# Attention, then a routed expert layer on one core: token rows scattered to expert regions batch by batch, in place of an inverse permutation built from one-hots

## The chip, the core and the metric

The kernel runs on one core of a Trainium2 chip. A core has five engines that run at the same time and meet through semaphores: TensorE (PE; its weight loads are listed as PEld), VectorE (DVE), ScalarE (ACT), GpSimd (POOL) and SyncE (SP), which issues transfers. Each engine takes its own instructions strictly in the order in which they were built. Transfers run on 16 DMA engines, through queues. The metric is the device time of one execution in microseconds (us).

## The reference

The input is `q`, `k`, `v` of shape 8 x 8 x 576 x 64 (batch, head, token, width), a gate matrix 512 x 8, a local gate 512 x 1 and, for eight experts, `w1` of 512 x 1024 and `w2` of 1024 x 512.

1. Attention for each batch and head, scale 1/8. A token sees all tokens of its own block of 64 and of the blocks before it (9 blocks of 64).
2. The heads are joined: x is 8 x 576 x 512.
3. Routing, token by token and in order within a batch. `fresh` is the argmax of the eight gate logits. The first token of a batch, and every token whose local gate is under 0.5, takes `fresh`; any other token keeps the expert of the token before it.
4. out = p[e] * (relu(x @ w1[e]) @ w2[e]), where p is the softmax of the gate logits and e the token's expert.

4,608 tokens go to 8 experts; how many go to each is known only at run time.

## The kernel before, in words

**Attention.** There are 32 pairs of heads (four pairs to a batch) and a loop over i from -1 to 31. Iteration i turns the exponentials of pair i (`turn_p`, L519), makes the scores of pair i+1 (`scores`, L481, three groups), their row maxima on DVE (`maxima`, L505) and exponentials on ACT (`exps`, L513), turns q and k of pair i+2 (`turn`, L462), finishes pair i-1 (`finish`, L569: five matmuls that transpose the output and give gate logits, then four DVE multiplications by the inverse row sums `rv`), and multiplies by v (`attend`, L544; `inverse`, L560, computes `rv` with six reciprocals on DVE). The order of all of these within an engine is the program's order (`pin`). `finish` adds the logits on POOL to `lg_all` and writes the token rows through SP to the DRAM tensor `x_rows`. Sixteen weight loads `w_bf` (1 MB each) are issued from POOL behind `finish`, one every one or two iterations (L634).

**Routing** (`routing`, L145) is a generator of small steps. Part 0 covers batches 0 to 5 at once, part 1 the last two. MIDDLE and BEHIND (L601, L602) say after which iterations 24 to 31 a step of part 0 is taken; MIDDLE is between `finish` and the third score group, BEHIND after `inverse`. A step finds the argmax, carries the kept expert along the tokens by a scan (over two round trips through DRAM on SP's queue), ranks the tokens of each expert by matmuls with a triangle and with ones, and gives each token a slot in a list of tiles of 128 tokens, each of one expert. The inverse (slot to token) is then built by one-hots: per batch a 128 x 640 comparison on DVE (L336), a narrower one (L339), five multiplications (L343) and matmuls (L350), which give token number and gate value of each slot.

**Expert layer.** 43 tiles (20 of part 0, 23 of part 1). For each: an indirect gather of 128 rows from `x_rows` on POOL (L665), four transposes (`turn_x`, L671), a DVE copy `xb` (L677), a DVE copy of the expert's `w1` into `wt` (`fetch`, L687), 32 matmuls (`up`, L694), two relus, the second of them on DVE from tile 18 on (L706 to L709), eight matmuls (`down`, L711), an ACT scaling into `o_sb` (four buffers, L719), and an indirect scatter to the output on POOL (L720). Part 1's routing steps stand between the first tiles (L742), without `pin`. Each output scatter waits until the one before it has landed, since both write one DRAM tensor.

Of the kernel before, what the change touches and what calls it, by code (L numbers as in the profile page):

```python
# [16 lines left out]
def kernel(  # L17
# [11 lines left out]
    nc = tc.nc  # L29
# [38 lines left out]
    lg_all = w_p.tile([P, B * NJ, E + 1], F32, tag="lg_all", name="lg_all")  # L68

    x_dram = nc.dram_tensor("x_rows", [BS, Dm], BF16).ap()  # L70
# [4 lines left out]


    NB0 = 6
    NC0 = NB0 * NJ
    NT0 = -(-(NB0 * S - E * (P - 1)) // P)
    PARTS = [(0, NC0, NT0), (NC0, NC_, NT - NT0)]  # L80
    NTM = max(NT0, NT - NT0)

    OUT = 8192.0
# [12 lines left out]
    K = Const()  # L96

    def route_constants():
        K.id_b = rt([P, P], BF16, "id_b")
        nc.gpsimd.tensor_copy(K.id_b, id_f)  # L100
        K.iota_e = rt([P, E], F32, "iota_e")
        nc.gpsimd.iota(K.iota_e, pattern=[[1, E]], base=0, channel_multiplier=0,
                       allow_small_or_imprecise_dtypes=True)
        K.desc_e = rt([P, E], F32, "desc_e")
        nc.gpsimd.tensor_scalar(K.desc_e, K.iota_e, -1.0, float(E), op0=ALU.mult, op1=ALU.add)
        K.thr = rt([P, NTM], BF16, "thr")
        nc.gpsimd.iota(K.thr, pattern=[[1, NTM]], base=0, channel_multiplier=0,
                       allow_small_or_imprecise_dtypes=True)
        K.iota_lo = rt([P, P], BF16, "iota_lo")
        nc.gpsimd.iota(K.iota_lo, pattern=[[1, P]], base=0, channel_multiplier=0,  # L110
                       allow_small_or_imprecise_dtypes=True)
        K.ones_b = rt([P, P], BF16, "ones_b")
        nc.gpsimd.memset(K.ones_b, 1.0)

        tri_f = rt([P, P], F32, "tri_f", tag="big")
        nc.gpsimd.memset(tri_f, 1.0)
        nc.gpsimd.affine_select(out=tri_f, in_=tri_f, compare_op=ALU.is_gt, fill=0.0,
                                base=0, pattern=[[1, P]], channel_multiplier=-1)
        K.tri_b = rt([P, P], BF16, "tri_b")
        nc.gpsimd.tensor_copy(K.tri_b, tri_f)  # L120
        K.ones_e = rt([P, NC0 * E], BF16, "ones_e")
        nc.gpsimd.memset(K.ones_e, 1.0)

        K.val = rt([P, NC_, 5], BF16, "val")
        tmp = rt([P, NC_], F32, "chunk_id", tag="eqm")
        nc.gpsimd.iota(tmp, pattern=[[S // 64, B], [2, NJ]], base=0, channel_multiplier=0,
                       allow_small_or_imprecise_dtypes=True)
        nc.gpsimd.tensor_copy(K.val[:, :, 0], tmp)
        tmp = rt([P, 1], F32, "part1", tag="mx")
        nc.gpsimd.iota(tmp, pattern=[[0, 1]], base=1, channel_multiplier=1,  # L130
                       allow_small_or_imprecise_dtypes=True)
        nc.gpsimd.tensor_copy(K.val[:, :, 1], tmp.to_broadcast([P, NC_]))
        K.oh = rt([P, E, NC_], BF16, "oh")
        K.slot = rt([P, NC_], F32, "slot")
        K.off = rt([P, E], F32, "off")
        K.sub = rt([P, E], F32, "sub")
        K.taken = rt([P, E], F32, "taken")
        K.cnt = rt([P, E], F32, "cnt")

    pslots = [rt([P, x[2]], F32, "pslot%d" % k) for k, x in enumerate(PARTS)]  # L140
    tok_gs = [rt([P, x[2]], I32, "tok_g%d" % k) for k, x in enumerate(PARTS)]
    tok_ss = [rt([P, x[2]], I32, "tok_s%d" % k) for k, x in enumerate(PARTS)]
    te_is = [rt([1, x[2]], I32, "te_i%d" % k) for k, x in enumerate(PARTS)]

    def routing(k, ew, last, psum, pin):  # L145

        c0, c1, nt = PARTS[k]
        n = c1 - c0
        b0, b1 = c0 // NJ, c1 // NJ
        a_dram = nc.dram_tensor("a_dram%d" % k, [2, b1 - b0, NJ * P], BF16).ap()  # L150
        e_dram = nc.dram_tensor("e_dram%d" % k, [b1 - b0, NJ * P], BF16).ap()
        dve = nc.vector
        rows = [P, n, E]

        def ts(out, in_, a, b, op0=ALU.mult, op1=ALU.add):
            pin(dve.tensor_scalar(out, in_, a, b, op0=op0, op1=op1))

        def each(ap):
            return ap[:, :, None].to_broadcast([P, E, n])

        lg = lg_all[:, c0:c1, :E]
        mx = rt([P, n], F32, "mx")
        pin(dve.reduce_max(mx, lg, axis=AX))
        mx3 = mx[:, :, None].to_broadcast(rows)

        eqm = rt(rows, F32, "eqm")
        pin(dve.tensor_tensor(eqm, lg, mx3, op=ALU.is_ge))
        pin(ew.tensor_mul(eqm, eqm, K.desc_e[:, None, :].to_broadcast(rows)))
        ep = rt(rows, F32, "ep")
        pin(ew.tensor_sub(ep, lg, mx3))  # L170
# [3 lines left out]
        best = rt([P, n], F32, "best")  # L174
        pin(dve.reduce_max(best, eqm, axis=AX))
        ak = rt([P, 2, n], F32, "ak")
        pin(dve.tensor_single_scalar(ak[:, 1, :], lg_all[:, c0:c1, E], 0.0, op=ALU.is_ge))
        pin(dve.memset(ak[0:1, 1, 0:n:NJ], 0.0))
        ts(best, best, -1.0, float(E))
        nkeep = rt([P, n], F32, "nkeep")  # L180
        ts(nkeep, ak[:, 1, :], -1.0, 1.0)
        pin(dve.tensor_mul(ak[:, 0, :], best, nkeep))
# [5 lines left out]
        pin(nc.tensor.transpose(ps[:2 * n, :P], ak.rearrange("p a c -> p (a c)"), id_f))  # L188
        akT = rt([2 * n, P], BF16, "akT")
        pin(nc.scalar.copy(akT, ps[:2 * n, :P]))  # L190
        nc.sync.dma_start(out=a_dram.rearrange("a b (t p) -> (a b t) p", p=P), in_=akT)
        row = rt([b1 - b0, 2, S], BF16, "row", tag="ring", bufs=2)
        nc.sync.dma_start(out=row, in_=a_dram[:, :, :S].rearrange("a b s -> b a s"))
        sm = rt([P, n], F32, "sm")
# [5 lines left out]
        erow = rt([b1 - b0, NJ * P], BF16, "erow", tag="ring", bufs=2)  # L200
        pin(dve.memset(erow[:, S:], 0.0))
        pin(dve.tensor_tensor_scan(erow[:, :S], row[:, 1, :], row[:, 0, :], 0.0,
                                   op0=ALU.mult, op1=ALU.add))
        nc.sync.dma_start(out=e_dram, in_=erow)
        ecr = rt([n, P], BF16, "ecr", tag="akT")
        nc.sync.dma_start(out=ecr, in_=e_dram.rearrange("b (t p) -> (b t) p", p=P))
        yield

        ps = psum()
        pin(nc.tensor.matmul(ps[:, :n], lhsT=ecr, rhs=K.id_b[:n, :n], start=True, stop=True))  # L210
        eix = rt([P, n], F32, "eix", tag="best")
        pin(dve.tensor_copy(eix, ps[:, :n]))

        oh = K.oh[:, :, c0:c1]
        pin(dve.tensor_tensor(oh, eix[:, None, :].to_broadcast([P, E, n]),
                              K.iota_e[:, :, None].to_broadcast([P, E, n]), op=ALU.is_equal))
        pin(dve.memset(K.oh[64:, :, c0 + NJ - 1:c1:NJ], 0.0))

        pin(ew.tensor_mul(ep, ep, oh.rearrange("p e c -> p c e")))
# [4 lines left out]
        for x, m in enumerate((K.tri_b, K.ones_b)):  # L224
            pin(nc.tensor.matmul(ps[:, x * n * E:(x + 1) * n * E].rearrange(
                "p (e c) -> p e c", e=E), lhsT=m, rhs=oh, start=True, stop=True))
        rc = rt([P, 2, E, n], F32, "rc", tag="big")
        rc2 = rc.rearrange("p x e c -> p (x e c)")
        pin(nc.scalar.copy(rc2, ps[:, :2 * n * E]))
        pg = rt([P, n], F32, "pg")  # L230
        pin(dve.reduce_sum(pg, ep, axis=AX))
        pin(dve.tensor_mul(pg, pg, sm))
        pin(dve.tensor_copy(K.val[:, c0:c1, 2], pg))
        for j in (3, 4):
            pin(dve.tensor_sub(pg, pg, K.val[:, c0:c1, j - 1]))
            pin(dve.tensor_copy(K.val[:, c0:c1, j], pg))
        yield

        inc = rt([P, E, n], F32, "inc", tag="eqm")
        pin(dve.tensor_tensor_scan(inc.rearrange("p e c -> p (e c)"), K.ones_e[:, :n * E],  # L240
                                   rc[:, 1].rearrange("p e c -> p (e c)"), 0.0,
                                   op0=ALU.mult, op1=ALU.add))

        pin(dve.tensor_sub(inc, inc, rc[:, 1]))
        pin(dve.tensor_add(rc[:, 0], rc[:, 0], inc))
        cnt = rt([P, E], F32, "cnt_n")
        pin(dve.tensor_add(cnt, inc[:, :, n - 1], rc[:, 1, :, n - 1]))
        pin(dve.tensor_sub(cnt, cnt, inc[:, :, 0]))
        yield

        ci = rt([P, 2, E], I32, "ci")
        til = rt([P, E], F32, "til")
        end = rt([P, E], F32, "end")
        exc = rt([P, E], F32, "exc")
        base = rt([P, E], F32, "base")

        def tiles(c):
# [525 lines left out]
```

## Time and profile before

| quantity | value |
|---|---|
| median of 3 runs | 623.67 us (623.26 to 628.08) |
| profiled execution: device time / span | 625.85 / 623.8 us |
| busy PE / DVE / ACT / POOL | 563.6 / 452.7 / 329.4 / 155.3 us |
| granted TensorE clock, mean | 0.975 |
| first matmul of the scores (L492) | 13.86 us |
| first `turn_p` (L526) | 23.55 us |
| one iteration, from 204 to 304 us | 11.9 us |
| first matmul of `up` (L700) | 429.81 us |
| `up` of the last tile / last output scatter issued | 605.23 / 616.45 us |

The span runs from the first to the last instruction of the profiled execution. An engine's busy time does not tell whether it sets the pace; that is read from what ends its idle time. Ends of matmuls are modelled, so starts are compared here.

### The profile page before, as it was taken

To read this page: it belongs to the slowest core of one execution; us is meant where nothing else is said; L and a number is where in the kernel's file an instruction comes from. 1 tells how busy PE (TensorE), PEld (TensorE's weight loads), DVE (VectorE), ACT (ScalarE), POOL (GpSimd) and SP (SyncE) were. 2 spreads that over 40 slices of the span, in tenths; PEclk is the share of its full clock that TensorE was granted. 3 is DMA by queue.
4 is the path that set the end of the run, shared out by engine and by line. 5 is a ranking of instruction groups with operands and counts; after the bars stand their busy time and mean duration, and the time that the engine had idled before them with its cause. 6 is when DMAs were issued, how large, how long until landed. Compare 5 with 4: busy or idle time off the path is not lost. (4 is left out here: it accounts for less than half of the span.)

```text
span 623.8 us, 15804 instructions
## 1 busy us (share of the span) xinstructions
PE 563.6 (90%) x5586; PEld 396.2 (64%) x5586; DVE 452.7 (73%) x1403; ACT 329.4 (53%) x1057; POOL 155.3 (25%) x218
## 2 busy tenths in 40 slices
PE   2899999999999999999999998765989899999991
PEld 1567667677677677666766665554667677766660
DVE  1688888888888888888888788894588855555540
ACT  1676676666666676666666765601444343323320
POOL 3000010010000001001010010144565565666532
PEclk9999999999999999999999999986999999999996
DMA  8246596595958668695874746102232222222210
GB/s 165 55 96 115 116 158 117 120 177 102 170 123 158 103 131 163 114 182 109 153 136 96 136 90 113 23 10 61 78 104 77 99 89 78 94 91 90 82 56 0
DMA packets 154078, 65.99 MB, mean 106 GB/s; under 512 B 138010, under 2 KB 146226, under 8 KB 154002
## 3 DMA queue, kind: packets, MB, share of 16 engines
q0 software_dynamic: 18048, 31.86, 24.8%
q1 hardware_dynamic: 132466, 32.52, 24.2%
q10 hardware_dynamic: 3488, 0.61, 0.6%
q8 instruction: 46, 0.75, 0.5%
q14 instruction: 30, 0.25, 0.1%
HBM read 67.55 MB, written 16.02 MB: 134 GB/s over the span
## 5 line engine op out<-in xcount | busy, mean ns | idle before, releaser
L516 ACT ACTIVATE pb<-ps_s,nm 128x512 f32<-128x512 f32 (+4 forms) x320 | 158.3, 501 | 97.8 <-DVE nm L508 97.3
L508 DVE TENSOR_REDUCE nm<-ps_s 128x1 f32<-128x512 f32 (+4 forms) x320 | 134.5, 453 | 54.0 <-ACT pb L516 31.8
L526 PE MATMUL ps_p<-id_f,pb 128*128 128x128 f32 (+1 forms) x800 | 105.1, 282 | 11.4 <-ACT pb L516 8.0
L492 PE MATMUL ps_s<-kT,qT 64*64 64x512 f32 (+7 forms) x1280 | 100.7, 419 | 6.1 <-ACT qT L475 6.1
L526 PEld LDWEIGHTS ps_p<-id_f,pb 128*128 128x128 f32 (+1 forms) x800 | 86.3, 141 | 24.7 <-ACT pb L516 10.0
L590 POOL TENSOR_TENSOR tmp<-tmp 128x45 f32<-128x45 f32 x32 | 8.5, 264 | 356.9 <-DVE tmp L582 356.9
L700 PEld LDWEIGHTS <-wt 128*128 128x128 bf16 x1376 | 81.1, 98 | 21.1 <-issue 15.8
L553 PE MATMUL ps_o<-pt,vt 128*64 128x320 f32 (+4 forms) x896 | 93.6, 360 | 0.0
L700 PE MATMUL ps_h<-xb,wt 128*128 128x128 bf16 x1376 | 84.3, 220 | 9.3 <-DVE xb L677 9.1
L714 PE MATMUL ps_o<-w_bf,hT 128*128 x344 | 86.6, 379 | 0.4
L553 PEld LDWEIGHTS ps_o<-pt,vt 128*64 128x64 f32 x896 | 59.3, 137 | 35.8 <-DVE tmp L582 4.9
L707 ACT ACTIVATE hT<-ps_h 128x512 bf16<-128x512 f32 x61 | 36.4, 597 | 79.1 <-PE ps_h L700 79.1
L720 POOL DMA_INDIRECT out_dram<-o_sb,tok_s x43 | 54.5, 1268 | 63.8 <-DMA out_dram<-o_sb,tok_s 21.0
L492 PEld LDWEIGHTS ps_s<-kT,qT 64*64 64x64 f32 x1280 | 45.4, 134 | 38.2 <-issue 23.6
L691 DVE COPY wt<-w_bf 128x4096 bf16 x43 | 53.1, 1238 | 15.5 <-PE ps_h L700 13.0
L516 ACT ACTIVATION_READ_ACCUMULATOR pb<-ps_s,nm 128x1 f32 x320 | 64.3, 201 | 0.0
L665 POOL DMA_INDIRECT xg<-x_rows,tok_g x43 | 55.3, 1286 | 22.6 <-PE ps_x L674 9.3
L719 ACT ACTIVATE o_sb<-ps_o,pslot 128x512 f32<-128x512 f32 x43 | 29.5, 687 | 44.0 <-PE ps_o L714 38.3
L709 DVE TENSOR_SCALAR hT<-ps_h 128x512 bf16<-128x512 f32 x25 | 17.3, 691 | 48.1 <-PE ps_h L700 48.1
L578 PE MATMUL ps_n<-wg,ot 128*128 128x146 f32 x320 | 49.4, 303 | 0.0
L541 ACT COPY pt<-ps_p 64x128 f32<-64x128 f32 (+2 forms) x102 | 43.6, 441 | 10.5 <-PE ps_p L526 10.3
L714 PEld LDWEIGHTS <-hT 128*128 128x128 bf16 x344 | 31.2, 98 | 24.8 <-issue 1.1
(147 smaller groups left out, 568.7 us busy)
## 6 DMA issues: line engine op xcount, KB each, us to landing
w_bf<-in_moe_w_dram POOLq DMA_DIRECT2D x16, 1024.0 KB, 10.2
natq<-in_q_dram SPq DMA_DIRECT2D x64, 128.0 KB, 2.6
vt<-in_v_dram SPq DMA_DIRECT2D x64, 128.0 KB, 4.7
natk<-in_k_dram SPq DMA_DIRECT2D x60, 128.0 KB, 2.7
x_rows<-xt SPq DMA_DIRECT2D x32, 128.0 KB, 2.6
natq<-in_q_dram SPq DMA_DIRECT2D x32, 32.0 KB, 2.5
vt<-in_v_dram SPq DMA_DIRECT2D x32, 32.0 KB, 6.3
natk<-in_k_dram SPq DMA_DIRECT2D x30, 32.0 KB, 2.2
```

The costliest lines, as they stand in the source:

```text
L492: pin(nc.tensor.matmul(ps[y][f * 64:(f + 1) * 64, c:c + n], lhsT=qT[r, i * 64:(i + 1) * 64], rhs=kT[r, a:a + n], start=True, stop=True))
L508: pin(nc.vector.reduce_max(nm[:, z:z + 1], ps[g][y][:, c:c + n], axis=AX, negate=True))
L516: pin(nc.scalar.activation(pb[i][:, a:a + n], ps[g][y][:, c:c + n], func=AF.Exp, bias=nm[:, i:i + 1], accum_out=rs[:, z:z + 1]))
L526: pin(nc.tensor.transpose(ps[:kk, (c + e) * P:(c + e + 1) * P], pb[i0 + 2 * e][:, j * P:j * P + kk], id128))
L541: pin(cp(dst, src))
L553: pin(nc.tensor.matmul(ps[h * D:(h + 1) * D, a - q0:qn], lhsT=vts[i % 3][:, j, h, :], rhs=pt[j][:, h, a - j * P:a - j * P + n], start=(j = ...
L578: pin(nc.tensor.matmul(ps[:, (t - t0) * (P + WG):(t - t0 + 1) * (P + WG)], lhsT=ot[:, t * P:(t + 1) * P], rhs=wg[:, hp], start=True, stop= ...
L665: nc.gpsimd.indirect_dma_start(out=xg[:], out_offset=None, in_=x_dram[:rows], in_offset=bass.IndirectOffsetOnAxis(ap=tok_gs[k][:, u:u + 1] ...
L691: nc.vector.tensor_copy(wt.rearrange("p k f -> p (k f)"), w1_bf[:, bass.ds(o, WE)])
L700: nc.tensor.matmul(ps_h[:, f, :], lhsT=wt[:, ko, fo * P:(fo + 1) * P], rhs=xb[:, ko * P:(ko + 1) * P], start=(ko == 0), stop=(ko == KO1 - 1))
L714: nc.tensor.matmul(ps_o, lhsT=hT[:, fo, :], rhs=w2_bf[:, bass.ds(woff + fo * Dm, Dm)], start=(fo == 0), stop=(fo == FO - 1))
L720: nc.gpsimd.indirect_dma_start(out=out_flat, out_offset=bass.IndirectOffsetOnAxis(ap=tok_ss[k][:, u:u + 1], axis=0), in_=o_sb[:], in_offse ...
```

## The change

Tokens are no longer sorted at the end; each batch's rows are put into place as soon as its routing is known.

* A DRAM tensor `x_sorted` (`xs`) holds one region of 4,608 rows for each expert. A row has 512 bf16 values, the token number and the gate value: 258 words.
* `finish` writes the token rows into an SBUF tile `x_b` of the batch (two buffers: batch b+2 takes the buffer of batch b), not to DRAM. The new `routing` runs once per batch, in nine steps that `hook` takes at nine places of the following iterations; `hook(i, 0)` stands where MIDDLE stood, `hook(i, 1)` where BEHIND stood. `K.free` holds the next free row of each region. The last two steps issue five indirect scatters (rows of 128 tokens) on POOL, L259.
* `table(0)` works out, from the counts of six batches alone, 16 tiles of full rows (part 0) and their row numbers; `table(1)` the other 27. A gathered row brings its token number and gate value along.
* The first three gathers are issued in iteration 30, the other 13 of part 0 right behind the last `finish`. Routing of batch 7 and the rest of batch 6 stand between the first tiles, on DVE.
* `inverse` makes one reciprocal on DVE and copies to `rv` with six POOL instructions. The v tiles have two buffers, not three. At the start the ACT queue issues three transfers, not ten, and loads the table of the exponential at once; gate weights and k of pair 1 go through SP. The second relu goes to DVE from tile 14.

In the built program, with the line numbers of the changed kernel, the five scatters c0 to c4 of a batch stand on POOL like this (batch 0; iteration 8 and the beginning of iteration 9):

```
L343 w_bf load
L259 c0
L532 L533 L534 L532 L533 L534   rv copies of pair 8; the fourth waits for c0's landing
L259 c1
L259 c2          waits for c1's landing
L169 L171 L173   step 1 of batch 1
L259 c3          waits for c2's landing
L259 c4          waits for c3's landing
L559 logits of finish(8)
```

For batches 1 and 2, c0 and c1 both stand ahead of the `rv` copies, and the fourth copy waits for c1. A `w_bf` load stands directly ahead of c0 for batches 0, 3, 4 and 5. On DVE, the first L554 of `finish` (pair 8 for batch 0) waits for the landing of all five scatters, since batch 2 takes the buffer of batch 0.

```diff
+    ROW = Dm // 2 + 2
+    xs = nc.dram_tensor("x_sorted", [E * BS, ROW], I32).ap()
+    PARTS = [NB0 * S // P - E - 3, 0]
+    PARTS[1] = NT - PARTS[0]
...
+    def gather(t, xg):
+        k, u = TILES[t]
+        nc.gpsimd.indirect_dma_start(
+            out=xg[:], out_offset=None, in_=xs,
+            in_offset=bass.IndirectOffsetOnAxis(ap=rows[k][:, u:u + 1], axis=0),
+            bounds_check=E * BS - 1, oob_is_err=False)
+        return xg
+    EARLY = 3
+    def gather_early():
+        for t in range(EARLY):
+            xgs.append(gather(t, rt([P, ROW], I32, "x_first", bufs=EARLY)))
+    def new_batch():
+        x = rt([P, NJ, ROW], I32, "x_b", bufs=2)
+        lg = rt([P, NJ, E + 1], F32, "lg", bufs=2)
+        return x, lg
+    def routing(b, x, lg, psum, pin, ew):
...
+        pin(dve.tensor_tensor_scan(row[:, 0, :S], row[:, 1, :S], row[:, 0, :S], 0.0,
+                                   op0=ALU.mult, op1=ALU.add))
...
+        pin(dve.tensor_add(rk[:, :NJ], rk[:, :NJ], K.free[:, None, :].to_broadcast(full)))
+        pin(dve.tensor_mul(rk[:, :NJ], rk[:, :NJ], oh))
+        to = rt([P, NJ], F32, "to")
+        pin(dve.reduce_sum(to, rk[:, :NJ], axis=AX))
+        to_i = rt([P, NJ], I32, "to_i", bufs=2)
+        pin(dve.tensor_copy(to_i, to))
+        pin(dve.memset(to_i[64:, NJ - 1:], E * BS))
+        pin(dve.tensor_add(K.free, K.free, rk[:, NJ]))
+        yield
+        for c in range(NJ):
+            pin(pool.indirect_dma_start(
+                out=xs, out_offset=bass.IndirectOffsetOnAxis(ap=to_i[:, c:c + 1], axis=0),
+                in_=x[:, c, :], in_offset=None, bounds_check=E * BS - 1, oob_is_err=False))
+            if c == 2:
+                yield
+        yield
+    def table(k, pin):
...
-        vts = [cst.tile([P, NJ, 2, D], F32, tag="v%d" % x, name="vt") for x in range(3)]
+        vts = [cst.tile([P, NJ, 2, D], F32, tag="v%d" % x, name="vt") for x in range(2)]
-                eng = nc.scalar if nm == "k" and i < 2 else nc.sync
+                eng = nc.scalar if nm == "k" and i == 0 else nc.sync
+        warm = rt([P, 1], F32, "warm")
+        nc.vector.memset(warm, 0.0)
+        pin(nc.scalar.activation(warm, warm, func=AF.Exp))
...
+            pin(nc.vector.reciprocal(rs[:, :NB], rs[:, :NB]))
             for f in range(2):
                 r = slice(f * 64, (f + 1) * 64)
-                pin(nc.vector.reciprocal(rv[:64, 0:1, f ^ swap[0]], rs[r, 0:1]))
-                pin(nc.vector.reciprocal(rv[:64, 1:, f ^ swap[2]], rs[r, 2:NB:2]))
-                pin(nc.vector.reciprocal(rv[64:, :NJ - 1, f ^ swap[1]], rs[r, 1:NB:2]))
+                pin(nc.gpsimd.tensor_copy(rv[:64, 0:1, f ^ swap[0]], rs[r, 0:1]))
+                pin(nc.gpsimd.tensor_copy(rv[:64, 1:, f ^ swap[2]], rs[r, 2:NB:2]))
+                pin(nc.gpsimd.tensor_copy(rv[64:, :NJ - 1, f ^ swap[1]], rs[r, 1:NB:2]))
...
                 pin(nc.vector.tensor_mul(
-                    xt[:, t0:t1].rearrange("p t (h d) -> p t h d", h=2),
+                    x.bitcast(BF16)[:, t0:t1, hp * P:(hp + 1) * P].rearrange("p t (h d) -> p t h d", h=2),
...
-            r = x_dram[b * S:(b + 1) * S, hp * P:(hp + 1) * P]
-            nc.sync.dma_start(out=r[:S4].rearrange("(t p) d -> p t d", p=P), in_=xt[:, 0:4, :])
-            nc.sync.dma_start(out=r[S4:], in_=xt[:S - S4, 4, :])
...
+        def hook(i, half):
+            if half == 1 and i % HP == 0 and i > 0:
+                b = i // HP - 1
+                steps[b] = routing(b, *batches[b], psum, pin, pool)
+                plan(steps[b], [(i, 1), (i + 1, 0), (i + 1, 1), (i + 2, 0), (i + 3, 0),
+                                (i + 3, 1), (i + 4, 0), (i + 4, 1), (i + 5, 0)])
+                if b == NB0 - 1:
+                    plan(table(0, pin), [(i + 4, 1), (i + 5, 0), (i + 5, 1)])
+            for x in todo.get((i, half), ()):
+                next(x, None)
+            if (i, half) == (HP * NB0 + HP + 2, 1):
+                gather_early()
...
-            if n == 0 or t < NT0 - 2:
+            if n == 0 or t < N0 - 2:
...
+        with tc.issue_after(gate_last.ins):
+            while len(xgs) < N0:
+                gather_next()
```

## The prediction

> **What bounds the kernel now.** First the slices of the span (15.6 us each): where PE and its granted clock both stand at 9, PE sets the pace; where both fall, something else does.
>
> ```profile
> PE   2899999999999999999999998765989899999991
> ...
> DVE  1688888888888888888888788894588855555540
> ...
> PEclk9999999999999999999999999986999999999996
> ```
>
> PE is full through attention, so there a delay costs time only once it reaches PE. The hole is in the slices 25 to 28 (374 to 436 us), the handover to the experts. Second, busy time by stretches there (columns: stretch; length; busy us and count of PE, PEld, DVE, ACT, POOL; granted clock; DMA share; GB/s):
>
> ```profile
> 400.00:410.00 10.00, 6.80 (x63) 5.62 (x65) 8.78 (x33) 4.41 (x17) 4.50 (x13) 1.00 0.06 15
> 410.00:420.00 10.00, 5.32 (x44) 4.45 (x40) 9.13 (x39) 0.00 (x0) 4.20 (x10) 0.75 0.01 3
> 420.00:430.00 10.00, 1.47 (x12) 0.94 (x11) 4.93 (x18) 0.27 (x1) 5.72 (x6) 0.50 0.20 51
> ```
>
> DVE carries this stretch with the one-hots, and PE waits. The last iterations and this hole are what the change can win. Third, what an attention iteration leaves over, PE's instructions in order of time (start, duration, engine, line; in brackets the idle time before and what ended it):
>
> ```profile
> 213.04 3.19 PE L526 MATMUL ps_p<-id_f,pb 128*128 128x128 f32 x25
> ...
> 386.81 5.02 PE L526 MATMUL ps_p<-id_f,pb 128*128 128x128 f32 x25 [1.97 <-ACT pb L516]
> ```
>
> The same 25 transposes took 5.02 after PE had idled 1.97 us, with a granted clock of 0.50 from 388 to 390: a stall costs itself and 1.84 more. Fourth, POOL's end, because the change scatters in a chain as the output does:
>
> ```profile
> 610.75 0.98 POOL L720 DMA_INDIRECT out_dram<-o_sb,tok_s  x1 [1.89 <-DMA out_dram<-o_sb,tok_s]
> 613.60 0.98 POOL L720 DMA_INDIRECT out_dram<-o_sb,tok_s  x1 [1.87 <-issue]
> 616.45 0.98 POOL L720 DMA_INDIRECT out_dram<-o_sb,tok_s  x1 [1.87 <-DMA out_dram<-o_sb,tok_s]
> ```
>
> One link of such a chain is 0.98 + 1.87 = 2.85 us. Fifth, issues and landings:
>
> ```profile
> q0 software_dynamic: 18048, 31.86, 24.8%
> ...
> w_bf<-in_moe_w_dram POOLq DMA_DIRECT2D x16, 1024.0 KB, 10.2
> natq<-in_q_dram SPq DMA_DIRECT2D x64, 128.0 KB, 2.6
> vt<-in_v_dram SPq DMA_DIRECT2D x64, 128.0 KB, 4.7
> ```
>
> All that POOL issues goes through q0, and a weight load needs 10.2 us to land.
>
> **The change, part by part**, against the profiled span of 623.8 (its device time was 625.85; the median of 623.67 is the span within 0.2, so the sum is read as a median without any correction).
>
> *Start: -5.5.* The first scores (13.86) wait for qT (ACT, 13.10), which stands behind the exponential's table load (11.81, 1.28 long), and that behind ten issues on ACT's queue, the last ending at 11.77. With three issues (to 2.65) the table is in by about 4. kT is then last: DVE's second copy starts at 7.81 and takes 0.49, so scores at 8.3.
>
> *Handover: -23.7.* From iteration 24 on, part 0's routing vanishes. `finish` of iteration 23 starts on DVE at 304.44; eight iterations of 11.9 without routing put the `attend` of pair 31 at 399.3 (it ended at 411.1). Behind it: copies, reciprocal, `rv`, gate matmuls and multiplications 3.9 (rows 410.81 to 420.85 without the one-hots and the waits for them), two `fetch` and an `xb` on DVE (1.22, 1.22, 0.42): 6.8. The first `up` comes at 406.1, not 429.81: the gathers already lie in SBUF, while before the chain was one-hots to 419.3, token rows written, gather at 423.90, transposes at 428.32.
>
> *Routing steps, spread over the iterations: +14.5.* The old scan of 6 rows took 1.31 us, and 1 row of the same 576 elements takes as long. DVE's steps between `finish` and the third score group are about 0.8, 1.45 (scan), 0.3 and 1.0 us per batch. The exponentials were ready 0.6 before PE's 213.04, so what exceeds 0.6 counts: 0.2 + 0.85 + 0 + 0.4 = 1.45 per batch, 9.7 for 6.7 batches. PE's added matmuls 0.4 each, 2.8; the table, some 15 small DVE operations of 0.17, about 2. Steps after `inverse` are covered by the five reciprocals saved (0.85); without that cover they cost up to 0.45 each, three to a batch, 9 in all. Before, iterations 24 to 28 grew by only 0.3 to 1.2 us for 0.8 to 1.5 of DVE's steps, so the whole lies between 10 and 25.
>
> *Waits for the scatters: +50.6.* This is a new wait. x_b has two buffers, so the first multiplication of `finish` of batch b+2 stands on DVE until all five scatters of batch b have landed; behind it on DVE are the maxima, without which ACT and then PE stop. It happens six times (iterations 9, 13, ..., 29). Let t be the start of `finish` in the iteration before. Row numbers are ready at t+2.0. The wait does no harm until t+13.05: one iteration, 0.13 to the multiplication, 0.6 of slack, 0.4 of idle that DVE has ahead of its later maxima. For batches 1 and 2: c0 at t+2.1, c1 at 4.95, landed 7.8, the held `rv` copies, c2 at 8.3, three links: 16.85. That is 3.8 late, twice: 7.6. For batches 0, 3, 4 and 5 a weight load is issued at about t+1.4, directly ahead of c0 in the same q0. If c0 waits for its 1 MB, it lands at 12.0, not at 5; `rv` copies 0.4; c1 at 12.4; four links: 23.8. That is 10.75 late, four times: 43. The other end is that the load holds nothing: c0 landed at 5, c1 at 6.5, the end at 17.9: 4.85 late each, 19.4, with the first two 27. No row of before has a scatter behind a load; the nearest is SP's v load, issued behind q and k: 4.7 against their 2.6. That is a transfer slowed by its forerunners in its queue, so I take the upper end. Behind the waiting POOL instructions stand the other three `rv` copies and, after c4, the logits of L559; `finish` needs `rv` at t+11.9, which the copies at 12.4 miss by less than its own wait, and the logits are needed a batch later.
>
> The page "DMA: Bandwidth & Descriptors" of the Trainium skill, section "Two DMAs through the same engine are not ordered", says that descriptors of one queue start in order; that would give the same upper end. Its section "Anatomy of one DMA — SWDGE (gpsimd) path" has a fit of 2.0 us plus the bytes over 436 per ns; for 132 KB that would be an estimate of 2.3 a link, against 2.85 in the rows above. By it the delays would be 1.1 and 8.5, this term 36 and the total 656. The measured link decides.
>
> *At nothing:* v tiles in two buffers (a load lands in 4.7 of an iteration's 11.9; if the cover were gone, `attend` would wait for the rest), the token rows no longer written (SP's transfers, 2.6 each, nobody waits for them until the first gather), gate weights through SP (first needed in `finish`, 10 us later).
>
> *Half clock behind each stall: +11.* Six times the 1.84 above, 0 if PE never idles long enough.
>
> *Experts: 0.* Tiles run at 4.27 (DVE rows 556 to 565: relu, `fetch`, `xb`, bound through PE) from 14 on, where before they ran at 3.83 up to tile 18 and some way on: 14 x 3.83 + 28 x 4.27 = 173.2 from first to last `up`, plus 4 for the routing still on DVE and 2.3 for 13 gathers (1.30 apart at 426 to 430) and ten chained scatters ahead of the output on POOL: 179.5 against 175.4. The backlog is bounded by 2, if `o_sb`'s four buffers cover it, and 13, if they do not. At the end no gathers stand between the last 17 output scatters, so POOL keeps up and the last is issued 1.9 after PE, not 6.0: -4.1.
>
> Sum: -5.5 - 23.7 + 14.5 + 50.6 + 11 + 4.1 - 4.1 = +46.9, so 670.
>
> **Rivals.**
>
> *The weight load doesn't hold c0.* For it: the 16 DMA engines are a quarter busy in q0, so scatters may pass between. Against: v behind q. The wait is 27, the sum 670.6 - 23.6 = 647 (632 with routing at 10 and no clock loss, 655 with routing at 22).
>
> *Faster: the scatters land inside the iteration.* A chain of five hides if the end is before t+13.05, that is (load not holding, c1 at 6.5) if a link is under (13.05 - 6.5) / 4 = 1.64 us. Then neither the wait nor the half clock is paid: 670.6 - 61.6 = 609. For it: the rows' 0.98 of descriptor work alone. Against: three links of 2.85 in a row, with an idle DMA around them.
>
> *Slower still.* The backlog on POOL at 13 and routing at 25: 670.6 + 10.7 + 10.5 = 692. For it: POOL has to start c0 to c4 of batch 6, 13 gathers and the first outputs in turn. Against: the four `o_sb` buffers give PE 4 x 4.27 = 17 us of tiles before it must wait for an output scatter.
>
> **How the numbers follow.** Forecast (655, routing at 10 and no clock loss, to 690, the backlog or the routing at its upper end and some of the other) 0.5, not held (632 to 655) 0.25, slower still 0.1, hidden 0.1, and 0.05 for a mixture that ends near no change. The range takes the first two and reaches to the third case's number, whose other half lies above: 632 to 692. A measurement of this kernel can't tell less than about 1% from no change (its three runs spread from 623.26 to 628.08). Faster by over 1%: 0.1; within 1%: 0.04; slower: 0.86.
>
> **What would show it.** In the profile after: DVE's multiplication in `finish` (L554) idle with the transfer of `x_sorted` as releaser, six times, about 4 us in iterations 13 and 17 and 11 in the others; POOL's L259 idle with the same releaser, starts 2.85 apart; clock below 9 in those slices; first scores near 8.3; the interval from the last `attend` to the first `up` near 7. Wrong if c0 lands about 3 us after its issue with the load in flight, if L554 shows no such releaser, or if iterations without a wait are over 14 us.

## The result, and the profile after

The changed kernel takes 734.32 us (median of 4 runs, 733.1 to 735.48) against 625.12 us beside it (4 runs, 623.26 to 628.08). The ratio is 1.174, with a 95% interval from 1.168 to 1.180. The forecast was 670, with a range of 632 to 692: the sign was right, the size was not. The profiled execution has a span of 731.4 us.

To see where 107.6 us came from, both spans are cut at the same five events, all read from the instructions in order of time. "Pair 0" and "pair 30" are the first DVE multiplication of `finish` of that pair (L582, now L551).

| stretch (us) | before | after | difference |
|---|---|---|---|
| start to `finish` of pair 0 | 42.6 | 37.9 | -4.8 |
| `finish` of pair 0 to that of pair 30 | 364.7 | 441.1 | +76.4 |
| from there to the first `up` | 22.4 | 9.5 | -12.9 |
| first `up` to the last tile's `up` | 175.4 | 218.4 | +42.9 |
| last tile's `up` to the end | 18.5 | 24.5 | +6.0 |

The slices of the changed kernel (now 18.3 us each) show the same at a glance:

```profile
PE   5999999579969969967994995877986786877980
...
DVE  3688888377758848737773874773731334333530
...
PEclk9999999979989979997997998799997999999995
```

Counted from 0, PE has six new dips in attention, at slices 7, 11, 14, 17, 21 and 24, each with a fall of the clock there or in the next slice, and through the expert layer, from slice 27 on, it is mostly at 6 to 8, where it was at 8 and 9.

The list of waits (engine, line and what it waited for; us in total, times, longest) names the waiters:

```profile
ACT o_sb L692 <- DMA out_dram<-o_sb,xg: 105.6, 26, 8.8
...
DVE x_b L554 <- DMA x_sorted<-x_b,to_i: 52.0, 6, 10.2
POOL x_sorted L259 <- DMA x_sorted<-x_b,to_i: 47.3, 24, 3.2
...
POOL rv L532 <- DMA x_sorted<-x_b,to_i: 20.6, 6, 5.3
...
ACT pb L480 <- POOL rv L534: 14.6, 5, 4.2
```

The second line is the wait that the forecast priced at 50.6 us. The first one, ACT waiting for a place to put its scaled output, belongs to the expert layer. The forecast named its buffers (`o_sb`) and bounded the backlog on POOL behind them at 13 us. The last one, ACT's exponentials waiting for the `rv` copies, was not in the forecast.

POOL in order of time, batch 0 (start, duration, engine, line; in brackets the idle time before and its releaser):

```profile
123.44 0.94 POOL L343 DMA_DIRECT2D w_bf<-in_moe_w_dram  x1
124.68 1.08 POOL L259 DMA_INDIRECT x_sorted<-x_b,to_i  x1 [0.31 <-DVE free L255]
...
134.35 0.18 POOL L532 COPY rv<-rs 64x1 f32<-64x1 f32 x1 [5.31 <-DMA x_sorted<-x_b,to_i]
...
135.16 1.02 POOL L259 DMA_INDIRECT x_sorted<-x_b,to_i  x1 [0.28 <-POOL rv L534]
138.55 0.98 POOL L259 DMA_INDIRECT x_sorted<-x_b,to_i  x1 [2.36 <-DMA x_sorted<-x_b,to_i]
...
141.58 1.01 POOL L259 DMA_INDIRECT x_sorted<-x_b,to_i  x1 [1.41 <-DMA x_sorted<-x_b,to_i]
145.61 0.97 POOL L259 DMA_INDIRECT x_sorted<-x_b,to_i  x1 [3.02 <-DMA x_sorted<-x_b,to_i]
```

The load is issued at 123.44, c0 at 124.68, and the copy that waits for c0 goes on at 134.35, 9.7 us after c0 was issued. In batch 1, without a load ahead, c0 and c1 start 3.27 apart. The links in the chain (start to start, those with `rv` copies between left out) are 3.39, 3.03 and 4.03 here and 3.27, 3.30 and 3.70 in batch 1: 3.45 on average, where the forecast had 2.85. On DVE, the six waits for the landing of the fifth scatter are these:

```profile
147.97 0.56 DVE L554 TENSOR_TENSOR x_b<-ps_n,rv 128x384 bf16<-128x384 f32 x1 [9.93 <-DMA x_sorted<-x_b,to_i]
205.68 0.56 DVE L554 TENSOR_TENSOR x_b<-ps_n,rv 128x384 bf16<-128x384 f32 x1 [6.47 <-DMA x_sorted<-x_b,to_i]
264.36 0.56 DVE L554 TENSOR_TENSOR x_b<-ps_n,rv 128x384 bf16<-128x384 f32 x1 [7.14 <-DMA x_sorted<-x_b,to_i]
329.90 0.56 DVE L554 TENSOR_TENSOR x_b<-ps_n,rv 128x384 bf16<-128x384 f32 x1 [10.21 <-DMA x_sorted<-x_b,to_i]
392.90 0.56 DVE L554 TENSOR_TENSOR x_b<-ps_n,rv 128x384 bf16<-128x384 f32 x1 [9.47 <-DMA x_sorted<-x_b,to_i]
454.27 0.56 DVE L554 TENSOR_TENSOR x_b<-ps_n,rv 128x384 bf16<-128x384 f32 x1 [8.76 <-DMA x_sorted<-x_b,to_i]
```

And POOL in the expert layer, gathers (L140) and output scatters (L693) in order of time:

```profile
604.06 1.58 POOL L140 DMA_INDIRECT xg<-x_sorted,rows  x1 [2.68 <-PE ps_h L674]
605.95 1.01 POOL L693 DMA_INDIRECT out_dram<-o_sb,xg  x1 [0.31 <-issue]
609.50 1.48 POOL L140 DMA_INDIRECT xg<-x_sorted,rows  x1 [2.53 <-PE ps_x L648]
611.28 1.01 POOL L693 DMA_INDIRECT out_dram<-o_sb,xg  x1 [0.31 <-issue]
```

Each gather stands idle for 2.5 us behind an output scatter, and each output scatter follows 0.31 us behind the gather: a loop of 5.4 us for a tile here (5.6 on average from 565 to 621 us), where PE and DVE need 4.27. The releaser that is printed at the gathers, a matmul, had long been done. In the built program the gather waits for the landing of the scatter ahead of it: that scatter takes its row numbers from a column of xg, and the gather wants that same buffer, 17 tiles on. POOL's order had been made so that every gather stands as early as its buffer allows, which is directly behind the output that frees it. Ahead of this loop nine gathers stand in front of two outputs, at 547 to 561 us; ACT's longest wait, 8.8 us, falls there.

### The profile page after: what moved, and what is told of

Read it like the earlier page. It is cut to its first block, busy times and chain, and to the rows that moved or that the text cites. A ratio compares the mean times of both kernels' runs of the same rounds, so it can differ in the third digit from the quotient of the medians.

```text
span 731.4 us, 15885 instructions
## 1 busy us (share of the span) xinstructions
PE 586.1 (80%) x5519; PEld 416.5 (57%) x5548; DVE 426.8 (58%) x1267; ACT 322.3 (44%) x1054; POOL 232.1 (32%) x488
## 5 line engine op out<-in xcount | busy, mean ns | idle before, releaser
L490 PE MATMUL ps_p<-id_f,pb 128*128 128x128 f32 (+1 forms) x800 | 116.3, 303 | 23.6 <-ACT pb L480 21.8
L490 PEld LDWEIGHTS ps_p<-id_f,pb 128*128 128x128 f32 (+1 forms) x800 | 98.5, 154 | 38.1 <-ACT pb L480 30.9
L674 PEld LDWEIGHTS <-wt 128*128 128x128 bf16 x1376 | 90.9, 106 | 24.7 <-issue 18.8
L674 PE MATMUL ps_h<-xb,wt 128*128 128x128 bf16 x1376 | 94.1, 233 | 10.5 <-DVE xb L651 6.2
L692 ACT ACTIVATE o_sb<-ps_o,xg 128x512 f32<-128x512 f32 x40 | 27.5, 687 | 124.4 <-DMA out_dram<-o_sb,xg 105.6
L140 POOL DMA_INDIRECT xg<-x_sorted,rows x40 | 50.2, 1256 | 55.9 <-PE ps_h L674 20.6
L693 POOL DMA_INDIRECT out_dram<-o_sb,xg x40 | 47.6, 1190 | 55.2 <-DMA out_dram<-o_sb,xg 28.1
L259 POOL DMA_INDIRECT x_sorted<-x_b,to_i x40 | 43.0, 1075 | 60.3 <-DMA x_sorted<-x_b,to_i 47.3
L554 DVE TENSOR_TENSOR x_b<-ps_n,rv 128x384 bf16<-128x384 f32 x64 | 30.9, 482 | 52.0 <-DMA x_sorted<-x_b,to_i 52.0
L503 DVE COPY pt<-ps_p 128x64 f32<-128x64 f32 (+2 forms) x192 | 43.6, 284 | 19.9 <-PE ps_p L490 19.1
L532 POOL COPY rv<-rs 64x1 f32<-64x1 f32 x64 | 11.9, 186 | 135.4 <-DVE rs L529 58.9
```

What stands on the lines that cost most here:

```text
L140: nc.gpsimd.indirect_dma_start(out=xg[:], out_offset=None, in_=xs, in_offset=bass.IndirectOffsetOnAxis(ap=rows[k][:, u:u + 1], axis=0), bo ...
L259: pin(pool.indirect_dma_start(out=xs, out_offset=bass.IndirectOffsetOnAxis(ap=to_i[:, c:c + 1], axis=0), in_=x[:, c, :], in_offset=None, b ...
L490: pin(nc.tensor.transpose(ps[:kk, (c + e) * P:(c + e + 1) * P], pb[i0 + 2 * e][:, j * P:j * P + kk], id128))
L503: pin(cp(dst[:, :, h], src[:, :, 1 - h]))
L674: nc.tensor.matmul(ps_h[:, f, :], lhsT=wt[:, ko, fo * P:(fo + 1) * P], rhs=xb[:, ko * P:(ko + 1) * P], start=(ko == 0), stop=(ko == KO1 - 1))
L693: nc.gpsimd.indirect_dma_start(out=out_flat, out_offset=bass.IndirectOffsetOnAxis(ap=xgs[t][:, Dm // 2:Dm // 2 + 1], axis=0), in_=o_sb[:], ...
```

## Experiments

Two theories were set against rivals: in attention, that the wait for x_b, lengthened by the weight load ahead of c0, is the loss; in the expert layer, that POOL's order and the late scatters are. The table has each run's stretches as above, beside the changed kernel's; the text has what follows. Each experiment but the sixth is one execution. In the expert layer the eighth run has the same order of instructions on POOL, PE and ACT as the changed kernel, and took 7.8 us more from the first to the sixteenth `xb` and 16.3 less from there to the last, 8.5 less in all. So a difference of this size in the last two stretches is not read from a single pair.

| kernel | to pair 0 | pair 0 to 30 | to first `up` | expert tiles | rest | span |
|---|---|---|---|---|---|---|
| changed | 37.9 | 441.1 | 9.5 | 218.4 | 24.5 | 731.4 |
| no early gathers | 37.0 | 441.2 | 13.5 | 221.0 | 15.1 | 727.8 |
| three x_b buffers | 37.1 | 385.6 | 13.7 | 220.5 | 21.7 | 678.4 |
| loads moved | 37.2 | 417.9 | 9.5 | 214.8 | 28.1 | 707.5 |
| gathers reordered | 36.9 | 441.6 | 9.5 | 198.1 | 20.3 | 706.4 |
| the three together | 37.6 | 372.3 | 13.5 | 202.2 | 21.0 | 646.6 |
| before, start and inverse | 38.2 | 357.6 | 22.2 | 183.4 | 14.7 | 616.0 |
| index copied | 37.2 | 440.4 | 9.5 | 233.6 | 13.9 | 734.6 |
| three row-sum buffers | 36.9 | 442.2 | 9.5 | 209.8 | 24.6 | 723.0 |
| no late scatters | 36.9 | 440.3 | 9.5 | 178.4 | 19.8 | 684.9 |

**No early gathers (control).** A third x_b buffer needs 5.2 KB in each partition, which the three early tiles and some sharing free.

```diff
-    EARLY = 3
+    EARLY = 0
-        ge = rt(full, F32, "ge", tag="big")
+        ge = rt(full, BF16, "ge", tag="big")
-        ecr = rt([NJ, P], BF16, "ecr")
+        ecr = rt([NJ, P], BF16, "ecr", tag="akT")
-        prod = rt(full, F32, "prod", tag="prod")
+        prod = rt(full, F32, "prod", tag="row")
```

> A control for the next run, which needs room in SBUF: no gather is issued in iteration 30 (all 16 of part 0 behind the last finish), and three small routing tiles share their place. Both theories: attention as in the changed kernel (first `up` near 488 there), the first gather with its landing stands bare, +3 to +5 us at the handover, so 734 to 739. If the early gathers hid more than that, over 740.

Measured: 729.49 us (629.60 for the kernel before beside it). The early gathers hide 4.0 us at the handover, as expected; the last two stretches together are 6.8 shorter, so the total lies 4.5 below what was expected. Early gathers were not a cause of the loss.

**Three x_b buffers.**

```diff
-        x = rt([P, NJ, ROW], I32, "x_b", bufs=2)
+        x = rt([P, NJ, ROW], I32, "x_b", bufs=3)
```

> The control with three x_b buffers instead of two. Theory 1 (the wait of `finish` for the landing of the scatters is attention's main loss): DVE's 52 us at L554 vanish, with them 10 us of half clock, so 55 to 65 less than the control, about 672, first `up` near 430. Rival (the serial chain of scatters only moves its delay to the next waiter, the `rv` copies and the exponentials behind them, 14.6 us now): less than 30 us gained, over 705. The expert layer stays at about 218 us from first to last `up` in both.

Measured: 680.12 us, 49.4 less than the control; attention alone is 55.6 shorter (441.2 to 385.6). No L554 waits for a transfer any more. The total falls short of the first theory's 55 to 65, but the rival, under 30, is out. The control's six waits sum to 52.1; the 55.6 are a net figure, since the load still holds the `rv` copies in this kernel (14.3 us of ACT's waits), so the price of the half clock can't be read from them. In iterations 13 and 17, which no load lengthens, the control took 8.4 and 8.0 us longer than this kernel, 2.2 and 1.9 more than its waits there. The clock line of this kernel, in slices of 17.0 us, has three 8s in attention and no 7; its fall to 6 is the handover:

```profile
PEclk9999999989999999989989999668997999999996
```

What is left, 385.6 against 30 iterations of 11.7 (351), is the routing's own work and, in iterations 8 and 9, 20 and 21, 24, 25, 28 and 29, the weight load.

**Weight loads moved away from the scatters.**

```diff
-                while done < min(2 * E, 2 * E * i // (NPR - 3)):
+                if done < 2 * E and (i < 8 or i % HP in (2, 3)):
```

> The changed kernel with its 16 weight loads issued in iterations 1 to 7 and then only in iterations with i mod 4 = 2 or 3, so that none stands ahead of a batch's scatters. Theory 1 (c0 waits in its queue for the 1 MB ahead of it): the waits at L554 of batches 0, 3, 4, 5 fall from 9.9, 10.2, 9.5, 8.8 to the 6.5 to 7.1 of batches 1 and 2, and the iterations before them from 15.9, 15.5, 14.2, 14.1 to 13.0: 15 to 22 us less, 710 to 717. Rival (loads and scatters pass side by side, POOL's chain alone sets the landing): within 3 us of 731.

Measured: 709.25 us. Attention is 23.2 shorter; all six iterations ahead of a wait now take 12.9 to 13.7 us (15.9, 13.0, 13.0, 15.5, 14.2, 14.1 before), and the waits are 7.1, 6.7, 6.3, 6.8, 6.3 and 4.4. So a scatter that is issued behind a 1 MB load waits for it. The Trainium skill, "DMA: Bandwidth & Descriptors", section "Two DMAs through the same engine are not ordered", says that within one queue of one DMA engine descriptors start in order, which agrees with these rows: 9.7 us for c0 behind the load, 3.2 to 4.0 from c0 to c1 without (batches 1 and 2 of the changed kernel, and batches 0 to 5 here).

POOL of this kernel, batch 0, without the load:

```profile
123.85 1.10 POOL L259 DMA_INDIRECT x_sorted<-x_b,to_i  x1 [0.79 <-DVE free L255]
127.60 1.01 POOL L259 DMA_INDIRECT x_sorted<-x_b,to_i  x1 [2.65 <-DVE rs L529]
...
131.68 0.98 POOL L259 DMA_INDIRECT x_sorted<-x_b,to_i  x1 [0.28 <-POOL rv L534]
...
135.20 1.02 POOL L259 DMA_INDIRECT x_sorted<-x_b,to_i  x1 [1.91 <-DMA x_sorted<-x_b,to_i]
138.31 0.99 POOL L259 DMA_INDIRECT x_sorted<-x_b,to_i  x1 [2.09 <-DMA x_sorted<-x_b,to_i]
```

c0 to c4 take 14.5 us here and took 20.9 with the load.

**Gathers reordered.** Each gather from tile 16 on goes behind the output scatter of seven tiles before.

```diff
+                with tc.issue_after(outs[t - 7].ins):
+                    xgs.append(gather(t, x))
```

> The changed kernel with each gather of part 1 (tiles 16 to 42) issued on POOL behind the output scatter of seven tiles before, not as early as its buffer allows. Theory 1 (in the expert layer each gather waits for the landing of the output scatter that stands just before it, whose index column lies in the same xg buffer; one link scatter, landing 2.5, gather, scatter is 5.4 us): from tile 16 on the pace falls to DVE's 4.27, 20 to 25 us less, 705 to 712; the lag of the outputs from the first 16 tiles stays. Rival (POOL or the DMA queue is simply full, 43 gathers and 43 scatters of 128 whole rows): pace stays above 5, within 5 us of 731.

Measured: 708.13 us. Attention is unchanged, the expert tiles take 20.3 us less and the rest 4.2 less; from tile 16 to 42 the pace is 4.47 on average, where it was 5.16. Not all of that is the order: the eighth and the third run have POOL's old order here, and run at 4.56 and 4.72. Against the eighth run the expert tiles take 11.7 us less, against the third 16.7, and the rest is shorter by 4.2 and 7.8. POOL's rows now show a gather between two scatters, inside the time that the scatter needs to land:

```profile
602.71 1.03 POOL L140 DMA_INDIRECT xg<-x_sorted,rows  x1 [0.30 <-issue]
604.93 1.74 POOL L694 DMA_INDIRECT out_dram<-o_sb,xg  x1 [1.19 <-ACT hT L682]
606.97 1.03 POOL L140 DMA_INDIRECT xg<-x_sorted,rows  x1 [0.30 <-issue]
```

The gathers and scatters are as many as before, so POOL and the queue were not full. The order is a cause; its size, 12 to 20 us in the tiles, depends on which execution with the old order stands beside it.

**The three together.** The edits of the second, third and fourth run.

> Three x_b buffers, the moved weight loads and the reordered gathers together (on the control without early gathers). Theory 1 (three separate losses, which add up): 678 less 16 for the iterations that a load lengthens (8 and 9, 20 and 21, 24 and 25, 28 and 29: 15.7, 14.5, 15.4, 13.6, 14.2, 15.3, 14.2, 15.0 down to 13.0 and 12.5) less 20 for the order: 642, with 635 to 650 as bounds. Rival (with a third buffer nobody waits for the scatters, so the loads no longer matter): 658. In either case still slower than the kernel before.

Measured: 648.35 us (629.96 for the kernel before beside it). Attention adds up: 441.2 to 372.3, of which the loads are 13.3 on top of the third buffer, so the rival falls: without a wait at L554 the load still holds the `rv` copies and `finish` behind them. An iteration with routing now takes 12.6, 12.2, 13.0 and 12.5 in turn, against 11.7 without: 21.3 us in all for the routing. It is slower than the kernel before still.

**The kernel before, with the start and the inverse alone.**

```diff
-                eng = nc.scalar if nm == "k" and i < 2 else nc.sync
+                eng = nc.scalar if nm == "k" and i == 0 else nc.sync
+        pin(nc.scalar.activation(warm, warm, func=AF.Exp))
-            nc.scalar.dma_start(out=wg[r, :, c:c + E], in_=gsrc[h])
+            nc.sync.dma_start(out=wg[r, :, c:c + E], in_=gsrc[h])
...
-                pin(nc.vector.reciprocal(rv[:64, 0:1, f ^ swap[0]], rs[r, 0:1]))
+                pin(nc.gpsimd.tensor_copy(rv[:64, 0:1, f ^ swap[0]], rs[r, 0:1]))
```

> The kernel before, with two small parts of the change alone: three transfers instead of ten on ACT's queue with the table loaded at once, and one reciprocal on DVE with six POOL copies to `rv`. Theory 1 (DVE's copies of `pt` stand behind the reciprocals and pace PE's transposes, 3.19 us before and 3.00 after): first scores at 8.5 instead of 13.86, and 0.19 less in each of some 30 iterations: 11 us less, ratio 0.982. Rival (PE is full in an iteration; the 11.7 us of the changed kernel come from the token rows that are no longer written to DRAM): only the 5.3 of the start, ratio 0.9915.

Measured: 617.93 us (4 runs, 616.32 to 618.38) against 629.96 (7 runs): ratio 0.981, 95% interval 0.979 to 0.984. The first scores come at 8.54, and quiet iterations take 11.7. PE in order of time:

```profile
65.37 3.00 PE L529 MATMUL ps_p<-id_f,pb 128*128 128x128 f32 x25
```

The transposes that the kernel before listed at 3.19 take 3.00. PE was listed as busy in all of its 11.9 us, and still it was being paced by DVE's copies. The token rows still go to DRAM in this version, so the rival falls. It beats both kernels, the one before by 1.9%.

**Token number and gate copied out of xg.**

```diff
+            meta = f_p.tile([P, 2], I32, tag="meta", name="meta", bufs=16)
+            nc.vector.tensor_copy(meta.bitcast(mybir.dt.uint16), xgs[t].bitcast(mybir.dt.uint16)[:, Dm:])
-                    ap=xgs[t][:, Dm // 2:Dm // 2 + 1], axis=0),
+                    ap=metas[t][:, 0:1], axis=0),
```

> The changed kernel, with token number and gate of each tile copied by DVE from the gathered rows into a small tile of 16 buffers, so that scaling and output scatter don't read xg. Theory 1 (a gather waits for the landing of the output scatter that reads its buffer): no gather has an output scatter as releaser any more; the pace from tile 16 on falls to 4.3 to 4.5, with 0.15 more on DVE per tile: 15 to 25 us less, 706 to 716. Rival (POOL or the queue is full): pace above 5, within 5 us of 731.

Measured: 736.44 us, a miss. The dependence was gone, as expected, but the time was not:

```profile
580.66 1.03 POOL L140 DMA_INDIRECT xg<-x_sorted,rows  x1 [4.89 <-PE ps_x L648]
582.00 1.02 POOL L693 DMA_INDIRECT out_dram<-o_sb,meta  x1 [0.31 <-issue]
```

With the buffers freed sooner, gathers were ordered still further ahead (20 output scatters stand behind the last gather, not 17). Now a gather waits for the transposes of the tile 17 before, and an old output scatter, which PE itself is waiting for through `o_sb`, stands behind it. So not the shared buffer by itself is the cause, but that an early gather waits ahead of a late output in one engine's order; the fourth run, which changed the order alone, is the one that shows it.

**Three buffers for the row sums.**

```diff
-                rs = rss[n] = o_p.tile([P, NB + 1], F32, tag="rs", name="rs")
+                rs = rss[n] = o_p.tile([P, NB + 1], F32, tag="rs", name="rs", bufs=3)
```

> The changed kernel with three buffers for the row sums, so that ACT's exponentials of the next pair no longer wait for the `rv` copies on POOL that stand behind a scatter (14.6 us in five waits). Theory 1 (the landing of the last scatter sets the end of the iteration, and this wait only takes part of the one at L554 ahead): L554's waits grow by what ACT's lose, 0 to 4 us less, 727 to 731. Rival (the two waits add up): 12 to 15 us less, 717.

Measured: 724.70 us. The total lies between the two expectations, but the stretches decide: attention is 442.2 against 441.1. The first wait at L554 went from 9.93 to 13.06 while the iteration ahead went from 15.9 to 13.3, and the sum of the six from 52.0 to 58.4. The wait of ACT was part of the same delay, only taken earlier. The other 8.5 us come from the expert layer (218.4 to 209.8), where POOL's instructions stand in exactly the same order as in the changed kernel; the last section has what the trace shows of that.

**No late scatters.** Batches 6 and 7 aren't scattered, on top of the reordered gathers.

```diff
-        for c in range(NJ):
+        for c in range(NJ if b < NB0 else 0):
...
-            in_offset=bass.IndirectOffsetOnAxis(ap=rows[k][:, u:u + 1], axis=0),
+            in_offset=bass.IndirectOffsetOnAxis(ap=rows[0][:, u % PARTS[0]:u % PARTS[0] + 1], axis=0),
```

> The kernel with reordered gathers, from which the ten scatters of batches 6 and 7 are left out; the tiles of part 1 gather rows of part 0 again, so the outputs of the last tokens are not the reference's. It shows what holds the first 15 tiles at 77.5 us from the first to the sixteenth `xb`, against 67.6 before. Theory 1 (the ten chained scatters keep POOL from the output scatters, and `o_sb` fills): 66 to 70. Rival (PE stands in its order behind the matmuls of the last two batches' routing, whose round trip through DRAM it waits for 3.7 us, and runs at half clock behind each such stop): 75 to 78, as with the scatters.

Measured: 686.59 us (626.13 beside it). From the first to the sixteenth `xb` 63.9 us, less than expected, and the expert tiles take 178.4 in all, 19.7 less than with the scatters. PE still waits once for the routing's round trip (2.57 us), so that rival is small. With order and late scatters both taken away, 3 us of the 42.9 are left.

How the 40 divide is less sure. From the second to the fourth `xb` the kernel with reordered gathers took 19.8 us, this one 11.3, and the fourth `xb` (507.7) lies ahead of the first scatter of batch 6 (508.42). So 8.5 of the 19.7 are not the late scatters'. The changed kernel had 11.3 there too, the third and the eighth run 19.9 and 19.6. The 8.5 us are idle time of PE, DVE and ACT for which no transfer is printed as releaser. From 496 to 500 us, first the changed kernel, then the one with reordered gathers:

```profile
496.00:500.00 4.00, 3.95 (x47) 2.92 (x46) 1.78 (x3) 2.12 (x5) 3.09 (x4) 1.00 0.34 94
496.00:500.00 4.00, 1.12 (x7) 0.50 (x6) 0.91 (x1) 1.19 (x2) 3.36 (x3) 1.00 0.36 99
```

(columns as in the forecast's stretches: busy us and count of PE, PEld, DVE, ACT, POOL; granted clock; DMA share; GB/s). What the engines waited for there is not known. Neither the changed kernel nor this one has it, so the sum of 40 stands; of it some 11 are the late scatters', and the rest is the order's, in the execution of the changed kernel that was profiled. The ninth run's late gathers don't need the late row numbers either; in the fourth run the first of them starts 0.30 us behind the output ahead of it, so it had not waited for them.

## Why the prediction went wrong

*Start, -5.5: right.* First scores at 8.53 (forecast 8.3).

*Handover, -23.7: about right.* The stretch is 12.9 shorter, and the kernel before had lost 7.7 in its iterations up to pair 30 (364.7 against 30 of 11.9), which is gone too: 20.6. The first `up` still waited 4.2 us for a routing step that stood ahead of it on DVE.

*Routing, +14.5 with 10 to 25: measured 21.3* from the run with all three edits. Each of the four iterations of a batch is longer, by 0.9, 0.5, 1.3 and 0.7: 3.3 for a batch, where the forecast had 1.45 on DVE and 0.4 on PE. Which of the steps it had counted as covered are not was not separated.

*Reciprocals: counted only as a cover, but worth -0.19 in each iteration.* The forecast read that PE is full through attention, and took it that work taken off DVE there gains nothing. The sixth run shows the gain by itself.

*Waits, +50.6, and half clock, +11: measured 68.9 together* (441.2 to 372.3 by buffer and loads). Iteration by iteration beside the kernel with all three edits, the six waits are 52.0, the iterations that have them lose 10.2 beyond the wait, and the iterations ahead of the four with a load are longer by 2.9, 2.6, 1.2 and 0.4, together 7.1. The place, the count and the load's share were right: of the two kinds, four waits of 10.75 and two of 3.8 were forecast and 9.9, 10.2, 9.5, 8.8 and 6.5, 7.1 came. That the four came so near is in part luck. The links were longer than forecast, but the held `rv` copies, which the forecast had put at nothing, made the iteration ahead longer and so gave the chain more time. In the eighth run, where ACT no longer waits for these copies, the four waits are 13.1, 11.4, 10.5 and 11.1.

The half clock came about as forecast. Behind the first wait PE's 25 transposes and the clock were

```profile
151.76 4.60 PE L490 MATMUL ps_p<-id_f,pb 128*128 128x128 f32 x25 [1.59 <-ACT pb L480]
152.00:154.00 2.00, 2.00 (x10) 1.71 (x10) 1.88 (x7) 0.63 (x5) 0.47 (x3) 0.50 0.01 1
```

(the second line is a stretch: PE busy for all of it, at a granted clock of 0.50). Behind the six waits these transposes took 31.6 us, and 22.4 in the same iterations of the kernel with all three edits: 9.2 of the 10.2.

The links were mis-sized. The three tail rows quoted in the forecast, 2.85 apart, are scatters that carry nothing: in the window from 604 us to the end the queue of the kernel before moved

```profile
q0 software_dynamic: 400, 0.00, 1.0%
```

(packets, MB, share of the 16 engines). The list of tiles is longer than the tiles with tokens, and unused slots are dropped. In the changed kernel unused slots repeat the last row, so every tile moves 256 KB; from 712 us to the end, five scatters, its queue moved

```profile
q0 software_dynamic: 400, 1.31, 17.7%
```

and POOL's last link is 0.98 + 2.60 = 3.58:

```profile
727.11 0.98 POOL L693 DMA_INDIRECT out_dram<-o_sb,xg  x1 [2.60 <-DMA out_dram<-o_sb,xg]
```

The fit of "DMA: Bandwidth & Descriptors" ("Anatomy of one DMA — SWDGE (gpsimd) path"), an estimate of 2.3 us for a scatter of 132 KB, lay further off still from the 3.45 that the chain shows.

*Experts, +4.1 - 4.1: this is the step that failed; measured +42.9 and +6.0.* The forecast summed POOL's items and bounded the backlog at 13 us, by `o_sb`'s buffers and the spacing of the gathers. It did not follow POOL's order through the layer. Two things stand there. The gathers, each ahead of an old output scatter and behind the one that frees its buffer, cost 12 to 20 us of the tiles as measured, 29 if the unexplained 8.5 of the fourth run are left out, and 4.2 of the tail. The ten scatters of batches 6 and 7, a chain of some 3.5 us a link through which the output scatters have to find their way, cost some 11 (ninth run, without these 8.5). Together they are 40.0, and the ninth run's 178.4 from first to last `up`, without both, is near the forecast's 179.5.

The lag of the outputs shows it: the first output scatter starts 23.2 us after the first tile's `xb`, the sixteenth still 32.8 after its own, where the kernel before had 9 and 8. Of the first 23.2, 19.3 are there without the late scatters too (ninth run), behind the 13 gathers; there the lag falls to 12 by the eighth tile. The forecast named one scatter chain as the loss in attention, and put the same chain ahead of the outputs, with the 13 gathers, at 2.3. The tail, -4.1, had the sign wrong for the same reason: the lag never drained, 20.7 us at the last tile instead of 11.7.

The forecast's own errors sum up: 48.9 in the experts, 11.1 in attention and the handover, 0.7 at the start, the 60.7 between +46.9 and +107.6.

The rivals: the load does hold c0 (third run). The chain does not hide: at 3.45 a link is twice the 1.64 from which it would have. "Slower still" went the right way, at 692, with a bound of 13 for what was some 40 in the tiles.

## What to carry to other kernels

Follow each in-order engine's built sequence through the whole program before pricing a serial resource: a chain of transfers costs where something else has to pass it, not only where its result is used. When a scheduler puts early work as far ahead as buffers allow, more or sooner free buffers can put it in front of the work that frees them; for the gathers here the order had to change, not the buffer. Take the price of a transfer from rows that move its bytes: look at the bytes of the window before taking the shortest links there as the rule.

## What was unexpected of the hardware

The descriptor work of an indirect transfer on POOL took two durations. In the expert layer of the changed kernel 50 of them take 1.01 us on average (1.17 at most) when no `fetch` copy runs on DVE at the same time, and 33 that overlap one, some of them barely, take 1.53; the kernel before has 1.05 (49) and 1.58 (37), the kernel with reordered gathers 1.01 (57) and 1.74 (26). The Trainium skill, "SBUF — State Buffer", section "Who interferes with whom", says that a DVE copy in its two-port mode and GpSimd's descriptor work exclude each other. The rows agree in direction; no view here shows the copies' mode, and no run took the copies away, so the cause is argued, not shown. It may be a part of why the eighth run, with the same order on POOL, had a loop of 5.0 us for a tile on average (about 4.86 in most turns), where the changed kernel had 5.6: its gathers fell mostly beside the copies, with 1.02 to 1.03 each. What sets on which side of the copies they fall stays open.
